# Attention and two MLP layers on one core: q and k loaded two pairs ahead, and the shared tile's scores on the column halves of TensorE

## The chip, the cores and the metric

The kernel runs on one core of one Trainium2 chip. The metric is the device time of one execution in microseconds (us). The engines are TensorE (PE for its matmuls, PEld for its weight loads), VectorE (DVE), ScalarE (ACT), GpSimd (POOL) and SyncE (SP), which here only issues DMAs.

## The reference, cut to what matters

```python
# q, k, v: (2, 12, 448, 64) float32, i.e. 24 heads of 448 positions and 64 dimensions
scores = q @ k^T / 8                         # per head, causal mask
attn = exp(scores - max) / (sum + 1e-9)
x = attn @ v                                 # -> 896 tokens x 768
h = x @ w_in;  g = max(h, 0) + alpha * min(h, 0);  x = g @ w_out     # d_ff = 2048, weights in float64
h = x @ w_in2; g = 0 below -1, h above 1, (h + 1)^2 / 4 between;  out = g @ w_out2
```

## The kernel before, in words

The heads are worked in 12 pairs. Pair `p` has one tile `qk_raw` (128 partitions: 64 dimensions of each of its two heads; q and k side by side). The 448 query rows of a head are three tiles of 128 and a rest of 64. The two rests of a pair share one tile of 128 rows, the "shared tile": its scores come from `qdiag`, a 128x128 block-diagonal of the two heads' last 64 queries, against all of `k` (line 372). `qk_raw` has three buffers that go round, and so has `qdiag`; `v` has five.

The loop of line 489 is a pipeline written out by hand. In its turn `p` it issues, in this order: the scores of pair `p` (query tiles 0 and 1, then the shared tile), their exponentials, attention times v of pair `p-2` (`attnv`, lines 446 and 454, which writes each head to one half of the partitions), its evacuation to `x`, one step of preparing the first MLP weights (from turn 3 on, `prime`), transposes of pair `p-1` (line 430), scores and exponentials of query tile 2, more transposes, and the division by the sums (`norm`: POOL, with one reciprocal on DVE). Every engine executes its instructions in the order in which they were issued. The scores of a turn go into banks `s0` and `s1`, which DVE empties into `pexp` (line 383); the transposes go into banks that ACT and DVE empty together (line 439).

DMAs of q, k, v and of the weights are all issued by SP in the order of the code, apart from half of pair 0. At the end of turn `p` (lines 523 to 529) come q and k of pair `p+1`, with two small DMAs for its `qdiag`, then v of pair `p+1` in seven DMAs, and in turn 1 the first two weight chunks of 768 KB each (line 103). The first step of `prime` is `magnitude` (ACT, line 113), which reads weight chunk 0 in turn 3; chunk 1 is read by the same step in turn 9.

After the loop four MLP layers follow (`run_layer`, line 253 makes all of their products, in three passes of split weights and inputs). Turns 12 and 13, which have no scores, already mix in products of layer 1.

Of the kernel before, what the change touches and what calls it, by code (L numbers as in the profile page):

```python
# [22 lines left out]
def attention_moe_moe_kernel(ctx: ExitStack, tc: tile.TileContext, qk, v, w1, w2, w3, w4, alpha, out):  # L23
# [8 lines left out]
    nc = tc.nc  # L32
    NP, _, _, S = qk.shape
    NB = 2
    CP, D = v.shape[1], v.shape[-1]
# [30 lines left out]
    def warm_up():  # L66

        z = const.tile([128, 512], F32R, tag="zero", name="zero")
        nc.vector.memset(f32(z), 0.0)
        for _ in range(NWARM):  # L70
            ps = ps_o.tile([128, 512], F32, tag="o", name="warm_ps")
            nc.tensor.matmul(ps, lhsT=z[:, :128], rhs=z, start=True, stop=True)

    def constants():
        nc.vector.memset(half, 0.5)
        make_identity(nc, ident)
        for t, p0, n in ((mask, 0, Q), (mask_rest, 0, D), (mask_rest, D, D)):
            if p0 == 0:
                nc.gpsimd.memset(t, 0.0)
            d = t[p0:p0 + n, t.shape[1] - n:]  # L80
            nc.gpsimd.affine_select(
                out=d, in_=d, compare_op=ALU.is_ge, fill=MASK, base=0, pattern=[[-1, n]], channel_multiplier=1
            )


    class Weights:
# [82 lines left out]
        def next(self):  # L169
            self.n_used += 1  # L170
            return self.split.pop(self.n_used - 1)
# [66 lines left out]
    def new_banks():  # L238

        pools = (ps_s, "s0"), (ps_s, "s1"), (ps_s, "s2"), (ps_o, "o"), (ps_t, "t0"), (ps_t, "t1"), (ps_t, "t0"), (ps_t, "t1")  # L240
        while True:
            for pool, tag in pools:
                yield pool.tile([128, 512], F32, tag=tag, name="ps")
# [17 lines left out]
    def early_tiles(batches):  # L261

        for f, bs in enumerate(batches):
            ws = wts.next()
            ps = {b: new_tile() for b in bs}
            early[f] = ws, ps
            for k in range(KD - 1):
                products(ps, ws, x_t, k, k, k == 0, False)
                yield

    def run_layer(layer, late):

        if layer in (1, 3):
            mt, nch, kc, src = NF, 1, KD, x_t
        else:
            mt, nch, kc, src = NM, NC2, KC, g_t
        evac = {1: act_prelu, 2: evac_x, 3: act_quad, 4: evac_out}[layer]
        for m in range(mt):
            ps = {}
            for ch in range(nch):  # L280
                if layer == 1 and m in early:
                    ws, ps = early.pop(m)
                    products(ps, ws, src, kc - 1, kc - 1, False, True)
                else:
                    ws = wts.next()
                rest = {b: new_tile() for b in range(NB) if b not in ps} if ch == 0 else ps

                end = layer == 4 and m == mt - 1 and ch == nch - 1
                for group in [{b: p} for b, p in rest.items()] if end else [rest] if rest else []:
                    for k in range(kc):  # L290
                        kk = ch * kc + k
                        products(group, ws, src, k, kk, kk == 0, kk == nch * kc - 1)
                    if end:
                        interleave(*(evac(p, m, b) for b, p in group.items()), [])
                ps = {**ps, **rest}
                if wts.n_used > 1 and not early:
                    interleave(wts.split_ops(), late)
                    late = []
                    wts.load()
                    wts.magnitude()  # L300
            late = [] if end else [op for pair in zip(*(evac(ps[b], m, b) for b in range(NB))) for op in pair]
        return late


    class Attention:
# [51 lines left out]
        def scores(self, p, tiles):  # L357
            if 0 in tiles:
                self.pexp[p] = self.ap.tile([Q, 2, TRI], F32, tag="pexp", name="pexp", bufs=3)
                self.st[p] = self.ap.tile([Q, 2, 2 * NQ + 1], F32, tag="stat", name="stat", bufs=4)  # L360
            t = self.raw[p]
            if NQ in tiles:
                banks = [self.ps_s.tile([128, 512], F32, tag="s2", name="rest_ps")]
            else:
                banks = [self.ps_s.tile([128, 512], F32, tag=f"s{j}", name=f"s{j}_ps") for j in range(2)]
            off, todo = 0, []
            for i in tiles:
                for n, (e, col) in enumerate(self.rows(p, i)):
                    w = e.shape[1]
                    ps = banks[n][:, off:off + w]  # L370
                    if i == NQ:
                        nc.tensor.matmul(ps, lhsT=self.qdiag[p % 3], rhs=t[:, 1, :], start=True, stop=True)
                        todo.append((e, ps, mask_rest, col))
                    else:
                        h = slice(n * D, (n + 1) * D)
                        nc.tensor.matmul(  # L376
                            ps, lhsT=t[h, 0, i * Q:(i + 1) * Q], rhs=t[h, 1, :w], start=True, stop=True
                        )
                        todo.append((e, ps, mask[:, REST - w:], col))
                off += w  # L380

            for e, ps, m, col in todo:
                nc.vector.tensor_tensor_reduce(  # L383
                    out=e, in0=ps, in1=m, scale=-SCALE, scalar=3.0e38, op0=ALU.add, op1=ALU.min,
                    accum_out=self.st[p][:, 0, col:col + 1],
                )
# [76 lines left out]
    with tc.manual_schedule():  # L463
        wts = Weights()
        ps_s, ps_t, ps_o = (
            ctx.enter_context(tc.tile_pool(name=f"ps_{n}", bufs=b, space=PSUM))
            for n, b in (("s", 1), ("t", 2), ("o", 1))
        )
        banks = new_banks()
        with ExitStack() as pa:  # L470
            ap = pa.enter_context(tc.tile_pool(name="attn", bufs=2))
            at = Attention(ap, ps_s, ps_t, ps_o)
            at.zeros()
            at.load(0)
            warm_up()
            at.load(1)
            at.load_v(0)
            nc.sync.dma_start(out=alpha_sb, in_=alpha)
            constants()
            early = {}  # L480
            fill = early_tiles(((0, 1), (0,)))
            prime = wts.prime()
            PRIME = 3

            for p in range(NP + 2):
                new, mid, old = p < NP, 1 <= p <= NP, p >= 2  # L490

                def spare():
                    if not new:
                        next(prime, None)
                        next(fill, None)

                if new:
                    at.scores(p, (0, 1))
                    at.scores(p, (NQ,))
                    at.expo(p, (0, 1, NQ))  # L500
                spare()
                if old:
                    at.attnv(p - 2)
                    high, low = at.evac(p - 2)
                    high()
                if p >= PRIME:
                    next(prime, None)
                if mid:
                    at.transp(p - 1, (0, 1))
                if new:  # L510
                    at.scores(p, (2,))
                if old:
                    low()
                if new:
                    at.expo(p, (2,))
                spare()
                if mid:
                    at.transp(p - 1, (NQ,))
                    at.transp(p - 1, (2,))
                if new:  # L520
                    at.norm(p)
                spare()
                if 0 < p < NP - 1:
                    at.load(p + 1)
                if p + 1 < NP:
                    at.load_v(p + 1)
                if p == PRIME - 2:
                    wts.load()
                    wts.load()
            for _ in fill:  # L530
                pass
            for _ in prime:
                pass
        gpool = ctx.enter_context(tc.tile_pool(name="g", bufs=1))
        ep = ctx.enter_context(tc.tile_pool(name="ep", bufs=2))
        late = []
        for layer in (1, 2, 3, 4):
            late = run_layer(layer, late)
            if layer % 2 == 0:
                interleave(late, [])  # L540
                late = []
# [44 lines left out]
```

## Time and profile before

| | |
|---|---|
| median of 3 runs | 563.89 us (562.46 to 571.53) |
| the profiled execution's own time | 563.78 us |
| its span, first to last instruction | 561.9 us |
| PE / DVE / ACT / POOL busy | 97% / 74% / 43% / 24% of the span |
| mean granted TensorE clock | 0.993 of full speed |

A row of the trace below gives start and duration in us, the engine, the line and operation, what it writes and reads, how many instructions were merged into it, and in brackets how long the engine had been idle before and what ended that. "SPq" rows are DMA issues: their duration is the time to issue, not to transfer. One float32 matmul of the code appears as two records (two passes).

### The profile page before, as it was taken

The page shows a single profiled execution, that of the slowest core. Times are in us where ns is not written, and L with a number is a line of the kernel's source. Part 1 is how long each engine was busy: PE and PEld are TensorE (multiplying, and loading weights), DVE is VectorE, ACT ScalarE, POOL GpSimd, SP SyncE. Part 2 cuts the span into 40 slices and gives each one's busy share as a digit, 9 for nine tenths or more (in the row PEclk, how much of TensorE's full clock was granted, in tenths as well). Part 3 has the DMA queues.
Part 4 walks back from the last instruction along what each step waited for, and adds up shares of the span by engine and source line. Part 5 has one row for each costly group of instructions (what it writes and reads, how often), then busy time and mean ns, then how long its engine had stood idle before and what let it go on. Part 6 is the DMA issues. An engine that isn't in the chain of part 4 may idle for free.

```text
span 561.9 us, 8739 instructions
## 1 busy us (share of the span) xinstructions
PE 547.4 (97%) x3195; PEld 482.2 (86%) x3195; DVE 418.4 (74%) x797; ACT 240.6 (43%) x509; POOL 136.6 (24%) x179
## 2 busy tenths in 40 slices
PE   7699999999999999999999999999999999999997
PEld 3456667999999999999999999999999999999996
DVE  4569886888888998765765779888888867555740
ACT  5578984333333333322233345555555433222220
POOL 4526753133333331000000003333333300000000
PEclk9889999999999999999999999999999999999999
DMA  4544511333333223433333523333322244343421
GB/s 122 199 136 117 167 55 58 112 113 113 113 113 113 75 76 113 127 98 113 114 112 88 177 97 108 113 113 113 113 95 75 76 129 143 132 130 128 145 71 33
DMA packets 25674, 62.31 MB, mean 111 GB/s; under 512 B 5280, under 2 KB 13984, under 8 KB 25632
## 3 DMA queue, kind: packets, MB, share of 16 engines
q1 hardware_dynamic: 23760, 60.15, 34.5%
q10 hardware_dynamic: 1872, 1.61, 0.8%
q8 instruction: 25, 0.41, 0.3%
q14 instruction: 17, 0.14, 0.1%
HBM read 58.99 MB, written 2.75 MB: 110 GB/s over the span
## 4 chain that ended last, share of the span: by engine, by line
PE 84%; POOL 0%; DVE 0%; ACT 0%; issue 0%; ACTq 0%
PE ps L253 83%; PE o_ps L446 0%; PE t_ps L430 0%; POOL pexp L403 0%; PE o_ps L454 0%; DVE o_sb L226 0%; ACT o_sb L226 0%; ACTq L226 0%
## 5 line engine op out<-in xcount | busy, mean ns | idle before, releaser
L253 PE MATMUL ps<-x,w_split 128*128 128x448 f32 x1152 | 234.7, 366 | 0.0
L253 PE MATMUL ps<-g,w_split 128*128 128x448 f32 x1152 | 233.8, 365 | 0.0
L253 PEld LDWEIGHTS ps<-g,w_split 128*128 128x128 f32 x1152 | 216.3, 188 | 17.1
L253 PEld LDWEIGHTS ps<-x,w_split 128*128 128x128 f32 x1152 | 216.0, 188 | 17.4
L177 POOL TENSOR_TENSOR g<-act_g,g 128x448 fp32r<-128x448 f32 x64 | 85.5, 1336 | 271.3 <-ACT g L176 271.2
L150 ACT CAST w_split<-w_f 128x512 fp32r<-128x512 f32 (+1 forms) x80 | 56.6, 707 | 125.8 <-DVE w_f L147 86.7
L153 DVE TENSOR_TENSOR w_split<-w_f,w_split 128x512 fp32r<-128x512 f32 (+1 forms) x80 | 66.1, 827 | 52.6 <-ACT w_split L150 52.5
L176 ACT CAST g<-act_g 128x448 fp32r<-128x448 f32 x64 | 36.2, 565 | 76.8 <-DVE act_g L189 62.8
L129 DVE TENSOR_SCALAR w_f<-w_f 128x512 f32<-128x512 f32 (+1 forms) x80 | 58.5, 731 | 9.0 <-ACT w_f L113 8.9
L147 DVE SCALAR_TENSOR_TENSOR w_f<-w_raw,w_f 128x512 uint32<-128x512 uint32 (+1 forms) x80 | 63.6, 795 | 1.4
L141 DVE SCALAR_TENSOR_TENSOR w_f<-w_raw,w_f 128x512 uint32<-128x512 uint32 (+1 forms) x80 | 63.5, 794 | 1.4
L113 ACT ACTIVATE w_f<-w_raw 128x512 f32<-128x512 f32 (+1 forms) x80 | 61.2, 764 | 0.4 <-DMA w_raw<-w 0.4
L392 ACT ACTIVATE pexp<-pexp,stat 128x128 f32<-128x128 f32 (+2 forms) x72 | 35.8, 499 | 16.8 <-DVE stat L383 16.5
L135 DVE TENSOR_SCALAR w_f<-w_f 128x512 uint32<-128x512 uint32 (+1 forms) x80 | 38.2, 478 | 1.4
L201 ACT ACTIVATE act_t<-act_t,half 128x448 f32<-128x448 f32 x32 | 21.5, 672 | 37.7 <-DVE act_t L200 37.7
L403 POOL TENSOR_SCALAR pexp<-pexp,stat 128x128 f32<-128x128 f32 (+2 forms) x72 | 34.5, 494 | 4.7 <-DVE stat L383 3.3
L383 DVE CUSTOM_DVE_ANT_0 pexp<-s_ps,mask 128x128 f32<-128x128 f32 (+2 forms) x72 | 26.2, 413 | 9.6 <-PE s_ps L376 9.2
L376 PE MATMUL s_ps<-qk_raw 64*128 64x128 f32 (+2 forms) x144 | 25.4, 431 | 5.6 <-DMA qk_raw<-qk 4.8
L226 DVE COPY o_sb<-ps 128x224 f32<-128x224 f32 x12 | 4.7, 391 | 29.8 <-ACT o_sb L226 29.8
L439 DVE COPY pt<-t_ps 128x128 f32<-128x128 f32 (+2 forms) x36 | 14.0, 418 | 13.1 <-PE t_ps L430 13.1
L446 PEld LDWEIGHTS o_ps<-pt,v 128*64 128x64 f32 x144 | 9.7, 143 | 14.9 <-ACT pt L439 6.0
L200 DVE TENSOR_SCALAR act_t<-ps 128x448 f32<-128x448 f32 x32 | 19.9, 622 | 3.0 <-PE ps L253 2.4
(47 smaller groups left out, 280.4 us busy)
## 6 DMA issues: line engine op xcount, KB each, us to landing
w_raw<-w SPq DMA_DIRECT2D x32, 768.0 KB, 4.3
w_raw<-w SPq DMA_DIRECT2D x48, 512.0 KB, 3.7
qk_raw<-qk SPq DMA_DIRECT2D x11, 448.0 KB, 3.9
out<-o_sb SPq DMA_DIRECT2D x12, 112.0 KB, 1.7
out<-o_sb ACTq DMA_DIRECT2D x12, 112.0 KB, 1.7
v<-v SPq DMA_DIRECT2D x12, 56.0 KB, 2.7
v<-v SPq DMA_DIRECT2D x12, 48.0 KB, 2.1
v<-v SPq DMA_DIRECT2D x12, 40.0 KB, 2.0
```

The lines of the kernel that those rows point to most:

```text
L113: nc.scalar.activation(out=f32(w), in_=f32(hi), func=AF.Abs)
L129: nc.vector.tensor_scalar(out=f32(w), in0=f32(w), scalar1=HI_MIN, scalar2=HI_MAX, op0=ALU.max, op1=ALU.min)
L135: nc.vector.tensor_scalar(out=w, in0=w, scalar1=5, scalar2=2, op0=ALU.logical_shift_left, op1=ALU.logical_shift_right)
L141: nc.vector.scalar_tensor_tensor(out=w, in0=hi, scalar=0xC0000000, in1=w, op0=ALU.bitwise_and, op1=ALU.bitwise_or)
L147: nc.vector.scalar_tensor_tensor(out=w, in0=lo, scalar=29, in1=w, op0=ALU.logical_shift_right, op1=ALU.bitwise_or)
L150: nc.scalar.copy(s[:, 0, :n], f32(w))
L153: nc.vector.tensor_sub(s[:, 1, :n], f32(w), f32(s[:, 0, :n]))
L176: nc.scalar.copy(t[:, 0, :], g)
L177: nc.gpsimd.tensor_sub(t[:, 1, :], g, f32(t[:, 0, :]))
L253: nc.tensor.matmul(ps[b][:, :S], lhsT=ws[:, part, k * 128:(k + 1) * 128], rhs=src[b, kk][:, xp, :], start=first and part == 0 and xp == 0, ...
L392: nc.scalar.activation(out=e, in_=e, func=AF.Exp, bias=st[:, 0, col:col + 1], scale=-1.0, accum_out=st[:, 1, col:col + 1],)
L403: nc.gpsimd.tensor_scalar(out=e, in0=e, scalar1=sums[:, col:col + 1], scalar2=1.0, op0=ALU.mult, op1=ALU.mult)
```

## The change

At the end of turn `p` the kernel now issues q and k of pair `p+2` instead of `p+1`, from turn 0 on; v stays one pair ahead. The first two weight chunks are issued one each in turns 1 and 2, behind q, k and v of that turn, where both were issued in turn 1. Second, the one matmul of the shared tile's scores is made as two, each with one half of the columns of `qdiag` (one head), each writing one half of the partitions.

```diff
@@ scores
                     if i == NQ:
-                        nc.tensor.matmul(ps, lhsT=self.qdiag[p % 3], rhs=t[:, 1, :], start=True, stop=True)
+                        for j in range(2):
+                            h = slice(j * D, (j + 1) * D)
+                            nc.tensor.matmul(
+                                ps[h], lhsT=self.qdiag[p % 3][:, h], rhs=t[:, 1, :], start=True, stop=True
+                            )
                         todo.append((e, ps, mask_rest, col))
@@ the loop over pairs
                 spare()
-                if 0 < p < NP - 1:
-                    at.load(p + 1)
+                if p + 2 < NP:
+                    at.load(p + 2)
                 if p + 1 < NP:
                     at.load_v(p + 1)
-                if p == PRIME - 2:
-                    wts.load()
+                if p in (PRIME - 2, PRIME - 1):
                     wts.load()
```

SP's instructions before, from q and k of pair 2 on (`qk_raw_275` is pair 2, `qk_raw_393` pair 3; `v2_88` is v of pair 2; `w_raw` are weight chunks):

```order
L336 DMA qk_raw_275<-qk 128x896
L340 DMA qdiag2_85<-qk 64x64 x2
L348 DMA v2_88<-v 112x128
L348 DMA v2_88<-v 16x128
L348 DMA v2_88<-v 96x128
L348 DMA v2_88<-v 32x128
L348 DMA v2_88<-v 80x128
L348 DMA v2_88<-v 48x128
L348 DMA v2_88<-v 64x128
L103 DMA w_raw_286<-w1 128x1536
L103 DMA w_raw_288<-w1 128x1536
L336 DMA qk_raw_393<-qk 128x896
```

Pair 3 is issued behind v of pair 2 and two weight chunks. The same place of SP's order now (`qk_raw_281` is pair 3, `qk_raw_398` pair 4):

```order
L336 DMA qk_raw_281<-qk 128x896
L340 DMA qdiag0_83<-qk 64x64 x2
L348 DMA v2_88<-v 112x128
L348 DMA v2_88<-v 16x128
L348 DMA v2_88<-v 96x128
L348 DMA v2_88<-v 32x128
L348 DMA v2_88<-v 80x128
L348 DMA v2_88<-v 48x128
L348 DMA v2_88<-v 64x128
L103 DMA w_raw_292<-w1 128x1536
L336 DMA qk_raw_398<-qk 128x896
```

Pair 3 now stands ahead of v of pair 2 and of every weight chunk, and it is pair 4 that follows one chunk.

PE's instructions at the head of turn 3, before (`s_ps` are scores, `rest_ps` the shared tile, `o_ps` attention times v of pair 1):

```order
L376 MATMUL s_ps<-qk_raw 128x128 x2
L376 MATMUL s_ps<-qk_raw 128x256 x2
L372 MATMUL rest_ps<-qk_raw,qdiag_83 128x448
L446 MATMUL o_ps<-pt,v_87 64x2x3x64 x2
L446 MATMUL o_ps<-pt,v_87 64x2x2x64 x2
```

and now, five lines further down in the code:

```order
L381 MATMUL s_ps<-qk_raw 128x128 x2
L381 MATMUL s_ps<-qk_raw 128x256 x2
L375 MATMUL rest_ps<-qk_raw,qdiag_83 64x448 x2
L451 MATMUL o_ps<-pt,v_87 64x2x3x64 x2
L451 MATMUL o_ps<-pt,v_87 64x2x2x64 x2
```

One matmul of 128 rows of output became two of 64, in the same place, and nothing else moved on PE.

## Rows read from the trace of the kernel before

**Rows 1.** The chain that ended last: start, us, what.

```profile
96.13 462.29 PE ps L253 x2280
```

**Rows 2.** Stretches: busy us of each engine, then granted clock, DMA share, GB/s.

```profile
20.00:25.00 5.00, 1.36 (x24) 0.90 (x22) 3.10 (x10) 2.48 (x9) 2.18 (x7) 1.00 0.88 340
25.00:30.00 5.00, 3.89 (x12) 1.75 (x14) 1.61 (x9) 1.84 (x8) 1.64 (x3) 0.52 0.42 117
```

**Rows 3.** PE in order of time: turns 2 to 5, then 9 to 11.

```profile
16.51 1.02 PE L372 MATMUL rest_ps<-qk_raw,qdiag 128*128 128x448 f32 x2
...
20.75 0.61 PE L430 MATMUL t_ps<-ident,pexp 64*128 64x64 f32 x12
26.11 1.65 PE L376 MATMUL s_ps<-qk_raw 64*128 64x128 f32 x8 [4.75 <-DMA qk_raw<-qk]
27.69 1.86 PE L372 MATMUL rest_ps<-qk_raw,qdiag 128*128 128x448 f32 x2
...
35.92 1.02 PE L372 MATMUL rest_ps<-qk_raw,qdiag 128*128 128x448 f32 x2
...
42.05 1.02 PE L372 MATMUL rest_ps<-qk_raw,qdiag 128*128 128x448 f32 x2
...
66.75 1.02 PE L372 MATMUL rest_ps<-qk_raw,qdiag 128*128 128x448 f32 x2
...
73.14 1.02 PE L372 MATMUL rest_ps<-qk_raw,qdiag 128*128 128x448 f32 x2
...
79.27 1.02 PE L372 MATMUL rest_ps<-qk_raw,qdiag 128*128 128x448 f32 x2
```

**Rows 4.** SP in order of time: issues of v, q and k, and weights.

```profile
8.27 3.27 SPq L348 DMA_DIRECT2D v<-v  x7
11.59 0.58 SPq L336 DMA_DIRECT2D qk_raw<-qk  x1
...
13.45 3.43 SPq L348 DMA_DIRECT2D v<-v  x7
16.92 1.07 SPq L103 DMA_DIRECT2D w_raw<-w  x2
18.09 0.45 SPq L336 DMA_DIRECT2D qk_raw<-qk  x1
...
20.79 6.03 SPq L348 DMA_DIRECT2D v<-v  x7
```

**Rows 5.** Last line of the view of line 336: its DMAs, issue to landing.

```profile
DMA to landing us min/median/max: 3.5/3.9/7.9
```

**Rows 6.** Last line of the view of tile `w_raw`, first 100 us.

```profile
DMA to landing us min/median/max: 4.2/4.6/7.1
```

**Rows 7.** Turn 5, in order of time: PEld waiting for DVE, DVE waiting for PE.

```profile
41.20 0.52 PEld L376 LDWEIGHTS s_ps<-qk_raw 64*128 64x128 f32 x6 [0.18 <-DVE stat L383]
...
45.57 0.62 DVE L439 COPY pt<-t_ps 128x128 f32<-128x128 f32 x2 [0.78 <-PE t_ps L430]
```

**Rows 8.** PE in very short stretches of turn 5: single records, and what follows.

```profile
42.53 0.54 PE L372 MATMUL rest_ps<-qk_raw,qdiag 128*128 128x448 f32 x1
43.00 0.54 PE L446 MATMUL o_ps<-pt,v 128*64 128x384 f32 x2
...
43.00 0.87 PE L446 MATMUL o_ps<-pt,v 128*64 128x384 f32 x4
```

**Rows 9.** PEld there in order of time.

```profile
43.37 0.14 PEld L446 LDWEIGHTS o_ps<-pt,v 128*64 128x64 f32 x2 [0.18 <-issue]
```

**Rows 10.** Turns 6, 7 and 9 in order of time: waiting transposes, and ACT's weight step.

```profile
53.00 0.52 PE L430 MATMUL t_ps<-ident,pexp 64*128 64x64 f32 x10 [0.19 <-POOL pexp L403]
...
59.30 0.68 PE L430 MATMUL t_ps<-ident,pexp 64*128 64x64 f32 x12 [0.60 <-POOL pexp L403]
...
70.38 0.92 ACT L113 ACTIVATE w_f<-w_raw 128x768 f32<-128x768 f32 x1
...
71.82 0.68 PE L430 MATMUL t_ps<-ident,pexp 64*128 64x64 f32 x12 [0.67 <-issue]
```

## The prediction

> **What bounds the kernel now.** First the chain that ended last: from 96.13 us on it is one piece, 2280 matmuls of the MLP layers with no gap, to the end of the work [rows 1]. So nothing after 96 us can be gained or lost by this change, unless it makes the weights late, and each microsecond that the attention part ends sooner or later moves the end by one microsecond.
>
> Next the busy time by stretches of 5 us over the attention part. One stretch stands out: from 20 to 25 us PE is busy for 1.36 us, while the DMA engines are 88% busy; in the next the granted clock has fallen to a mean of 0.52, that is, to the lower of its two levels, 1.2 GHz [rows 2]. PE in order of time shows what happened. It finished turn 2's transposes at 21.36 (20.75 + 0.61) and next ran the scores of pair 3 at 26.11, 4.75 us later, released by the DMA of q and k; the shared tile's scores, which follow, took 1.86 us instead of 1.02 [rows 3]. The step from one turn's shared tile to the next's is a clean yardstick: 42.05 - 35.92 = 6.13 us undisturbed, but 27.69 - 16.51 = 11.18 from turn 2 to 3 and 35.92 - 27.69 = 8.23 from turn 3 to 4 [rows 3].
>
> SP's order says why the DMA was late. Pair 3 was issued at 18.09, right behind two weight chunks at 16.92 [rows 4], and took 7.9 us to land, the longest of all q and k loads against a median of 3.9 [rows 5]: 18.09 + 7.9 = 26.0, which is where PE starts.
>
> Then what sets the 6.13 us. In turn 5 DVE stands idle for 0.78 us until PE's transposes are done, then copies them and empties the banks of query tile 2's scores; PE's next scores wait for that [rows 7]. After them PE runs the shared tile, attention times v and the transposes, on which DVE waits again. The shared tile lies on this loop, though not in every turn: in turns 6 and 7 the last transposes wait for POOL (0.19 and 0.60 us), in turn 9 they wait (0.67 us) behind ACT, whose order now holds the 0.92 us weight step of line 113 [rows 10].
>
> **The loads, step by step.** SP reaches pair 3 sooner: v of pair 1 began at 8.27, and pair 2, which took its place behind that at 11.59, now stands ahead of it. q, k and `qdiag` cost SP 13.45 - 11.59 = 1.86 us, v of a pair some 3.3 [rows 4]. So pair 2 is issued at 8.3, v of pair 1 at 10.1, pair 3 at about 13.4. Its buffer is that of pair 0, whose last scores PE makes before turn 1's shared tile, which stood a step ahead of 16.51, near 10.4; so SP does not wait for it. Even the longest landing gives 13.4 + 7.9 = 21.3 [rows 5], just when PE comes free at 21.36; a median one gives 17.3. Step 2 to 3 then is a normal 6.13: 11.18 - 6.13 = 5.05 us gained. In step 3 to 4 the clock stays at its upper level, but ACT has line 113 in turn 3, as in turn 9, and step 9 to 10 took 73.14 - 66.75 = 6.39 [rows 3, 10]: 8.23 - 6.39 = 1.84. Together **6.9 us**. Bounds: if both steps are 6.13, 7.2; if both are 6.39, 6.6.
>
> What is moved past what: v of pair 1 comes 1.9 us later, is all issued by 13.4 and is first read in turn 3, beyond 22 us, so hidden. v of pairs 2 and on stands where it stood. Weight chunk 0 comes at about 13.4 + 1.9 + 3.4 = 18.7 instead of 16.9. Its first reader is ACT in turn 3; in turn 9 this step began 70.38 - 66.75 = 3.63 after the shared tile [rows 3, 10], so it is wanted at 16.51 + 6.13 + 3.63 = 26.3. The longest landing of a weight chunk, 7.1 us [rows 6], gives 25.8: hidden, by 0.5 in the worst case. If that cover goes, ACT waits ahead of the copies that PE's transposes need, one for one. Chunk 1 comes some 6 us after chunk 0, at about 24.5, and is wanted in turn 9. Pair 4, issued right behind chunk 0 at 19.2, lands at 27.1 at the worst; turn 4 wants it at 21.4 + 6.4 = 27.8. Later SP runs a pair ahead and waits for PE to free the buffer of pair `p-1`; behind that wait stand v and the later chunks, each with turns to spare. What is late next in turn 3 is thus nothing on DMA, but DVE's emptying of the banks, as in every turn.
>
> **The halves, step by step.** Today the shared tile's two passes begin at 42.05 and 42.53, and attention times v at 43.00: 0.95 us of path [rows 3, 8]. Attention times v is already made on column halves. Its records of 384 columns come two side by side, and the second two end 0.87 - 0.54 = 0.33 us after the first two [rows 8]. By columns, 0.33 x 448 / 384 = 0.385 for each pass of the shared tile on both halves, 0.77 for both passes, with nothing paid between it and the attention matmuls, which stand in the same arrangement. That is **0.18 us less** on the loop of a turn. The weight loads double in number (four for two); their cover is the matmuls themselves, as with the two loads of 0.14 us that run at 43.37 under the matmuls of 43.00 to 43.87 [rows 8, 9].
>
> The step is followed by attention times v in ten turns, 2 to 11. In turns 3 and 9 ACT, in 6 and 7 POOL ends the wait last, and I count nothing there: 6 x 0.18 = **1.1 us**. Bounds: 0, if POOL, ACT and DVE take it up everywhere, and 10 x 0.18 = 1.8. I take 1.1, since DVE's 0.78 us of idle time in turn 5 says that it does have room.
>
> **The sum.** 6.9 + 1.1 = 8.0. The profiled execution took 563.78 us (span 561.9 and 1.9 around it), within 0.1 of the median of the three runs: 563.8 - 8.0 = **555.8 us**, 1.4% less.
>
> **Rivals.** *The halves give nothing.* POOL's division and ACT's copies stand 0.2 to 0.7 us behind PE in three turns of [rows 10]; a faster PE may only wait longer for them. For it: these waits. Against: the six turns without one. 563.8 - 6.9 = 556.9.
>
> *The weight loads of the halves are bare.* If none could run beside a matmul, each of the four pieces would have a load of 0.14 ahead of it: 0.77 + 0.56 = 1.33 for 0.95, or 10 x 0.38 = 3.8 lost: 563.8 - 6.9 + 3.8 = 560.7. Against: the loads at 43.37. The Trainium skill ("TensorE: Matmul & The Clock Gate", Part 3, The mechanism) states such a rule: a weight load overlaps a running matmul only where the two use different row groups, and the two halves here use the same rows. By that rule it would come out so; the trace differs, with loads under running matmuls of just this shape.
>
> *The halves run one after the other,* each as long as the shared tile today: 1.90 for 0.95, in ten turns 9.5 us, and the kernel is slower than before: 563.8 - 6.9 + 9.5 = 566.4. It decides from 6.9 / 10 = 0.69 us more per turn on. For it: both halves stream the same `k`, which no matmul pair here does. Against: the side-by-side records of [rows 8].
>
> *Pair 3 is late still,* since more small DMAs of v stand just ahead of it, or SP is held up: at half the loss (3.4 us) 560.3. Against: it needs a landing beyond 7.9 us with no weight chunk in the way.
>
> **Chances.** Forecast 0.60; halves give nothing 0.17; loads bare 0.05; one after the other 0.04; pair 3 late 0.04; both terms at their upper bounds, 563.8 - 9.0 = 554.8, or a little under, 0.10. The range takes in the forecast, the first and the last case. Its ends are the bounds of both terms, 554.8 and 563.8 - 6.6 = 557.2, each widened by 1.4 us, the distance of the fastest run from the median of those shown, to 553.4 and 558.6; I take 553.2 to 559.0. About 2% (11.3 us, below 552.6) is what a measurement of this kernel can tell from no change, and no case above goes that far either way: faster 0.05, the same 0.92, slower 0.03, where the tails stand for mechanisms that I have not seen.
>
> **What would show it.** Right: no idle PE between 21 and 26 us, granted clock 1.00 from 20 us on, q and k landing within some 5 us, turn 3's shared tile near 22.6 and turn 4's near 29; the last piece of the chain beginning near 88; the shared tile 0.77 us ahead of attention times v, with four records in two side-by-side pairs. Wrong: ACT waiting for `w_raw` in turn 3, transposes waiting longer for POOL, or a step between shared tiles of 6.13 still, which would make the halves worth nothing.

## The result, and the profile after

The changed kernel took 0.9869 of the time of the kernel before (95% interval 0.9846 to 0.9891). Its profiled execution took 555.52 us, span 553.7, where the one before took 563.78: 8.3 us less, against 8.0 forecast (555.8); by the ratio, over more executions, it is 1.3% less, against 1.4% forecast. Some executions of the kernel before, of the changed one and of others here are some 9 us longer or more, in the profiled ones because the 2280 matmuls of the MLP layers take 471.40 us instead of 462.29 at the same granted clock, and no run here tells why: ratios and ranges leave them out, and four profiles of this kind (the halves alone, v in two DMAs on the changed kernel, and both of the last version) are read for their attention part only.

The chain of waits of the changed kernel, its last long piece:

```profile
87.89 462.29 PE ps L253 x2280
```

It is as long as before and begins 96.13 - 87.89 = 8.24 us sooner [rows 1]: the whole gain lies ahead of it. The two stretches by 5 us that stood out before [rows 2], now:

```profile
20.00:25.00 5.00, 5.00 (x62) 3.22 (x60) 4.60 (x20) 4.29 (x17) 2.68 (x7) 1.00 0.78 272
25.00:30.00 5.00, 4.13 (x58) 2.67 (x56) 3.97 (x17) 4.81 (x17) 2.35 (x6) 1.00 0.50 150
```

PE is busy throughout the first, and the clock never leaves its upper level. PE in order of time, the rows that answer to [rows 3] and [rows 8]:

```profile
16.57 0.97 PE L375 MATMUL rest_ps<-qk_raw,qdiag 128*64 128x448 f32 x4
...
22.50 0.97 PE L375 MATMUL rest_ps<-qk_raw,qdiag 128*64 128x448 f32 x4
...
27.56 0.68 PE L435 MATMUL t_ps<-ident,pexp 64*128 64x64 f32 x12 [0.87 <-issue]
...
28.88 0.97 PE L375 MATMUL rest_ps<-qk_raw,qdiag 128*64 128x448 f32 x4
...
34.82 0.97 PE L375 MATMUL rest_ps<-qk_raw,qdiag 128*64 128x448 f32 x4
35.62 1.46 PE L451 MATMUL o_ps<-pt,v 128*64 128x384 f32 x12
...
71.23 0.97 PE L375 MATMUL rest_ps<-qk_raw,qdiag 128*64 128x448 f32 x4
```

Steps between shared tiles: turn 2 to 3 5.93 us (11.18 in [rows 3]), 3 to 4 6.38 (8.23), 4 to 5 5.94 (6.13). The shared tile now has four records, two side by side, and attention times v follows 0.80 us after its start, not 0.95. Turn 5 in very short stretches, first two of the records and then the four weight loads, done at 35.02 while those run:

```profile
34.82 0.60 PE L375 MATMUL rest_ps<-qk_raw,qdiag 128*64 128x448 f32 x2
...
34.82 0.20 PEld L375 LDWEIGHTS rest_ps<-qk_raw,qdiag 128*64 128x64 f32 x4 [0.33 <-DMA v<-v]
```

SP in order of time, for [rows 4], and the landing of q and k from the view of line 336, for [rows 5]:

```profile
8.29 0.43 SPq L336 DMA_DIRECT2D qk_raw<-qk  x1
...
13.52 0.53 SPq L336 DMA_DIRECT2D qk_raw<-qk  x1
...
19.05 1.38 SPq L103 DMA_DIRECT2D w_raw<-w  x1
20.52 0.38 SPq L336 DMA_DIRECT2D qk_raw<-qk  x1
...
27.32 0.39 SPq L336 DMA_DIRECT2D qk_raw<-qk  x1
...
34.05 0.35 SPq L336 DMA_DIRECT2D qk_raw<-qk  x1
...
40.54 0.53 SPq L336 DMA_DIRECT2D qk_raw<-qk  x1
...
46.12 0.53 SPq L336 DMA_DIRECT2D qk_raw<-qk  x1
```

```profile
DMA to landing us min/median/max: 3.0/4.0/5.4
```

Pair 3 was issued at 13.52, 7.7 us before its scores. But the later pairs are not a turn ahead: pair 7 was issued at 40.54 and its scores began at 45.94, 5.4 us later, which is just the longest landing; pair 8 came 5.58 us after it.

### The profile page after: what moved, and what is told of

Its sections match the earlier page's. It is cut to its first block, busy times and chain, and to the rows that moved or that the text cites. A ratio compares the mean times of both kernels' runs of the same rounds, so it can differ in the third digit from the quotient of the medians.

```text
span 553.7 us, 8785 instructions
## 1 busy us (share of the span) xinstructions
PE 543.2 (98%) x3219; PEld 480.8 (87%) x3219; DVE 418.2 (76%) x797; ACT 239.8 (43%) x509; POOL 136.8 (25%) x179
## 4 chain that ended last, share of the span: by engine, by line
PE 85%; POOL 0%; DVE 0%; ACT 0%; issue 0%; ACTq 0%
PE ps L253 84%; PE o_ps L451 0%; PE t_ps L435 0%; POOL pexp L408 0%; PE o_ps L459 0%; DVE o_sb L226 0%; ACT o_sb L226 0%; ACTq L226 0%
## 5 line engine op out<-in xcount | busy, mean ns | idle before, releaser
L381 PE MATMUL s_ps<-qk_raw 64*128 64x256 f32 (+2 forms) x144 | 25.1, 425 | 0.7 <-DVE stat L388 0.7
L184 DVE TENSOR_SCALAR act_t<-ps,alpha_sb 128x448 f32<-128x448 f32 x32 | 21.5, 672 | 0.1
```

## The experiments

**Each part alone.** The loads only (the shared tile undone):

```diff
-                        for j in range(2):
-                            h = slice(j * D, (j + 1) * D)
-                            nc.tensor.matmul(
-                                ps[h], lhsT=self.qdiag[p % 3][:, h], rhs=t[:, 1, :], start=True, stop=True
-                            )
+                        nc.tensor.matmul(ps, lhsT=self.qdiag[p % 3], rhs=t[:, 1, :], start=True, stop=True)
```

> Only the loads are changed; the shared tile is one matmul of 128 columns, as before. If the two parts simply add, as the prediction has it: 6.9 us less than the kernel before, 556.9 us by the profile (span about 555.0), shared-tile steps of 6.13 us from turn 2 to 3 and about 6.39 from 3 to 4, undisturbed steps still 6.13. If the loads are worth something only together with the halves: above 558.5 us.

Measured: 0.989 of the time before (0.9874 to 0.9907), 556.66 us profiled. PE in order of time:

```profile
16.29 1.02 PE L372 MATMUL rest_ps<-qk_raw,qdiag 128*128 128x448 f32 x2
...
22.42 1.02 PE L372 MATMUL rest_ps<-qk_raw,qdiag 128*128 128x448 f32 x2
...
28.82 1.02 PE L372 MATMUL rest_ps<-qk_raw,qdiag 128*128 128x448 f32 x2
34.95 1.02 PE L372 MATMUL rest_ps<-qk_raw,qdiag 128*128 128x448 f32 x2
```

Steps of 6.13, 6.40 and 6.13: the term of the loads as it was worked out.

The halves only (the kernel before with the new lines 372 to 376):

> Only the halves are changed; q and k one pair ahead and both weight chunks in turn 1, as before. If the halves pay by themselves: undisturbed steps of 5.94 us instead of 6.13, the steps 2 to 3 and 3 to 4 still around 11 and 8, in all about 1 to 1.3 us less than before, 562.5 to 562.8 us. If they pay only where the loads are early: 563.8 us.

Measured: 0.9976 (0.9966 to 0.9985), 562.19 us median. Compared at like granted clock, with the runs of the kernel before on that chip, the means differ by 1.1 us (0.991 to 0.994) and 1.6 us (0.996 and 0.997). The attention part of the profile has undisturbed steps of 5.94 us, and turn 3 still waits.

```profile
26.40 1.65 PE L380 MATMUL s_ps<-qk_raw 64*128 64x128 f32 x8 [4.86 <-DMA qk_raw<-qk]
...
34.91 0.97 PE L374 MATMUL rest_ps<-qk_raw,qdiag 128*64 128x448 f32 x4
40.85 0.97 PE L374 MATMUL rest_ps<-qk_raw,qdiag 128*64 128x448 f32 x4
46.79 0.97 PE L374 MATMUL rest_ps<-qk_raw,qdiag 128*64 128x448 f32 x4
```

So each part pays by itself and they add: 0.989 x 0.9976 = 0.9866.

**Which part of the new load order counts.** Both chunks in turn 1 again, the rest as changed:

```diff
-                if p in (PRIME - 2, PRIME - 1):
+                if p == PRIME - 2:
+                    wts.load()
                     wts.load()
```

> The changed kernel, but with both weight chunks issued in turn 1 again, behind v of pair 2; pair 4 then stands behind two chunks, where pair 3 stood before. If only the place of pair 3 matters: pair 4 is issued near 21 us and lands by 28 to 29, turn 4 wants it at 28.05, so 0 to 1 us more than the changed kernel, 555.5 to 556.5 us. If spreading the chunks over two turns is what pays: turn 4 waits for pair 4 as turn 3 did for pair 3, 3 us or more, 558.5 us or more.

Measured: 557.65 us, between the two. Step 3 to 4 took 7.67 us (6.38 as changed): pair 4, issued at 20.85, reaches 28.45 with this run's longest landing, 7.6 us, and its scores began at 28.63, though the view puts that wait down to DVE. And PE waited 1.58 us in a turn that nobody had named:

```profile
72.49 0.93 PE L381 MATMUL s_ps<-qk_raw 64*128 64x128 f32 x8 [1.58 <-DMA qk_raw<-qk]
```

This is pair 11, over 45 us after the chunks. One pair ahead, with the chunks moved behind pairs 3 and 4:

```diff
-                if p == PRIME - 2:
-                    wts.load()
+                if p in (PRIME - 1, PRIME):
                     wts.load()
```

> The kernel before (one pair ahead, one matmul for the shared tile), but with the two weight chunks issued in turns 2 and 3, one each, behind q, k and v of that turn. If what counts is that pair 3 stands ahead of the chunks: pair 3 is issued at 16.9 us and lands near 21, turn 3 starts on time or under 0.6 us late, and ACT waits at most 1 us for chunk 0: 556.9 to 558.5 us. If a lead of two pairs is needed: turn 3 still waits 2 us or more for pair 3, above 559.5 us.

Measured: 561.2 us, the second alternative by its total, though turn 3 itself was only 0.59 us late. PE and ACT in order of time:

```profile
21.77 0.93 PE L376 MATMUL s_ps<-qk_raw 64*128 64x128 f32 x8 [0.59 <-DMA qk_raw<-qk]
...
28.07 0.89 ACT L113 ACTIVATE w_f<-w_raw 128x768 f32<-128x768 f32 x1 [1.86 <-DMA w_raw<-w]
...
37.04 0.93 PE L376 MATMUL s_ps<-qk_raw 64*128 64x128 f32 x8 [1.39 <-DMA qk_raw<-qk]
...
69.74 0.93 PE L376 MATMUL s_ps<-qk_raw 64*128 64x128 f32 x8 [1.18 <-DMA qk_raw<-qk]
```

The waits are spread over the whole attention part. That pointed away from the two chunks alone and to SP, which in both kernels issues ten DMAs a pair. So the same kernel again, with v of a pair laid out in memory so that two DMAs bring it (in `load_v`):

```diff
-            k = 0
-            while k < S:
-                (c, r), (d, u) = divmod(k, Q), divmod(k, CP)
-                n = min(Q - r, CP - u)
-                nc.sync.dma_start(out=t[r:r + n, c], in_=v[p, u:u + n, d])
-                k += n
+            n = Q * NQ * 2 * D
+            nc.sync.dma_start(out=t[:, :NQ], in_=v[p, :n].rearrange("(r c j d) -> r c j d", r=Q, c=NQ, j=2))
+            nc.sync.dma_start(out=t[:D, NQ], in_=v[p, n:].rearrange("(r j d) -> r j d", r=D, j=2))
```

> The run with one pair ahead and the chunks in turns 2 and 3, with v of a pair in two DMAs instead of seven. If its late turns waited for q and k because SP, with ten DMAs a pair, issues them too late: no PE wait for q and k over 0.2 us any more, and ACT's wait for chunk 0 (1.86 us) mostly gone, 556.5 to 557.5 us. If one pair of lead is too little whatever SP does: the waits of turns 5, 7 and 10 stay, above 559 us.

Measured: 556.15 us, no wait of PE for q and k or of ACT for a chunk left, 5.05 us less for five DMAs fewer a pair; these are single executions, but their profiles agree, with the last piece of the chain beginning at 93.59 and at 88.56. That is as fast as the loads-only kernel above, without the second pair of lead in the code. The other layout also means fewer packets (7213 against 11246 in the first 90 us), so this run does not separate fewer issues from fewer packets. What it does show is that q and k landed no sooner after their issue (median 4.4 us against 4.0): they were issued sooner. SP now does run ahead, until a buffer is not free (it waits for PE for 22.7 us in 8 waits): in its order of time the issues are a turn apart, with pair 5 at 19.98 for its shared tile at 34.40, and pairs 6 and 7 behind it:

```profile
19.98 0.33 SPq L336 DMA_DIRECT2D qk_raw<-qk  x1
...
26.11 0.33 SPq L336 DMA_DIRECT2D qk_raw<-qk  x1
...
32.49 0.33 SPq L336 DMA_DIRECT2D qk_raw<-qk  x1
```

The same edit on the changed kernel:

> The changed kernel with v of a pair in two DMAs instead of seven (another layout of v in memory). If SP's issuing of some 6.2 us per turn only just keeps up in the changed kernel but costs it nothing: the time stays at 555.3 to 555.7 us, while q and k of each pair are issued over 8 us before their turn instead of 5.4 to 7.7. If it costs something already: below 555.0 us.

Measured, in the attention part: it ends at 87.51 us, against 87.89, with the same steps (5.94, 6.38, 5.94 ...) and pair 7 issued at 32.51, against 40.54. SP cost the changed kernel nothing in that profiled execution. But in another execution of the very same changed kernel it did:

> The changed kernel itself, on the same chip: 555.5 us, 0.6 to 1.0 us above the one with v in two DMAs and ACT's steps moved; from turn 2's shared tile to the last piece of the chain 71.3 us.

Measured: 0.9891 (0.9871 to 0.9911), 555.22 to 558.58 us; the profiled one took 556.54 and shows two waits and what stands behind the first:

```profile
27.06 0.58 SPq L103 DMA_DIRECT2D w_raw<-w  x1
27.74 0.38 SPq L336 DMA_DIRECT2D qk_raw<-qk  x1
...
34.29 0.93 PE L381 MATMUL s_ps<-qk_raw 64*128 64x128 f32 x8 [1.31 <-DMA qk_raw<-qk]
...
70.92 0.93 PE L381 MATMUL s_ps<-qk_raw 64*128 64x128 f32 x8 [0.51 <-DMA qk_raw<-qk]
```

Pair 5, right behind the second chunk, was issued 0.4 us later than in the first profile and took 6.4 us to land instead of at most 5.4. PE was also early: turn 2's shared tile began at 15.91, 0.66 us sooner than in the first profile, so part of the two waits is that lead given back, and the last piece of the chain began 1.05 us later (88.94). The expectation of a fixed 555.5 us fell: the changed kernel sits at the edge.

**Where the halves save.** The shared tile first in each turn, so that attention times v no longer follows it, once with halves and once with one matmul:

```diff
-                    at.scores(p, (0, 1))
                     at.scores(p, (NQ,))
-                    at.expo(p, (0, 1, NQ))
+                    at.scores(p, (0, 1))
+                    at.expo(p, (NQ, 0, 1))
```

> The changed kernel with the shared tile's scores, their reduction and their exponentials ahead of those of query tiles 0 and 1 in each turn. The shared tile then fills PE's wait for DVE's banks and leaves the loop of PE and DVE. If that loop is the only limit of a turn: undisturbed steps of 5.6 to 5.7 us instead of 5.94, about 552.5 us. If SP, which issues a pair's DMAs in about 6.2 us, is the next limit: PE waits for q and k again in late turns, the turns stay near 5.9 to 6.2, 554 to 556 us.

> The same order with the shared tile as one matmul on all 128 columns, so that it differs from the run before it only in the halves, and in neither does attention times v follow the shared tile. If the halves save because nothing is paid between the shared tile and attention times v: no difference here, the shared tile to the next scores within 0.05 us of the halves. If they save in the tile itself, by shorter weight loads: 0.1 to 0.2 us longer from the shared tile's start to the next scores' start than with halves.

Measured: 559.57 us with halves, 559.11 with one matmul. With halves it is the longer by what happened up to turn 3's shared tile (at 23.63 us against 22.95), where its granted clock averaged 0.66 from 15 to 20 us; from there to the last piece of the chain it is 0.22 us shorter (68.31 against 68.53). From shared tile to the next scores, PE in order of time, first with halves, then without:

```profile
36.49 0.97 PE L375 MATMUL rest_ps<-qk_raw,qdiag 128*64 128x448 f32 x4
37.40 0.93 PE L381 MATMUL s_ps<-qk_raw 64*128 64x128 f32 x8
```

```profile
35.85 1.02 PE L372 MATMUL rest_ps<-qk_raw,qdiag 128*128 128x448 f32 x2
36.80 0.93 PE L376 MATMUL s_ps<-qk_raw 64*128 64x128 f32 x8
```

0.91 against 0.95: away from attention times v the halves are worth 0.04 us, next to it 0.95 - 0.80 = 0.15. So, by the difference, most of the saving is what was not paid between the two, not the tile itself. As a faster kernel the order failed, and not in the way that either expectation had it: the undisturbed step did fall, to 5.78 us, without any wait for q and k, but the seven steps from turn 4 to 11 took 43.51 us against 42.35 in the changed kernel. In turn 7, for one, the transposes waited 0.93 us and began at 54.98, when ACT, held up by the cast of line 150, had made its copy (to 54.88). Why these waits grow is read from the trace, not tested.

**What the long turns wait for.** ACT's step of line 113 moved behind its first copy of transposes, turns 3 and 9:

```diff
-                if p >= PRIME:
+                if p >= PRIME and p not in (3, 9):
                     next(prime, None)
                 if mid:
                     at.transp(p - 1, (0, 1))
+                if p in (3, 9):
+                    next(prime, None)
```

> The changed kernel with ACT's weight step of line 113 issued behind ACT's first copy of transposes in turns 3 and 9, instead of ahead of it. If this step is what makes the steps 3 to 4 and 9 to 10 long (6.38 and 6.37 us): both fall to 5.94 to 6.1, 0.6 to 0.9 us less in all, 554.6 to 554.9 us. If it is the DMAs of these turns: both stay at 6.4, 555.5 us.

Measured: 555.37 us. Steps 3 to 4 and 9 to 10 fell to 5.93, but the steps after them rose from 5.94 to 6.11, so the two places gained 0.28 and 0.27 us, 0.55 in all, just short of the expectation; that ACT's 0.9 us still does not fit into its idle time would explain it, and was not tested. From turn 2's shared tile to the last piece of the chain 70.80 us, against 71.32.

Then both that and v in two DMAs, and in turn 7 ACT's cast of line 150 moved in the same way:

```diff
-                nc.scalar.copy(s[:, 0, :n], f32(w))
+                high = lambda: nc.scalar.copy(s[:, 0, :n], f32(w))
+                high() if self.defer is None else self.defer.append(high)
```

> The changed kernel with v in two DMAs, ACT's step of line 113 behind the first copy of transposes in turns 3 and 9, and its cast of line 150 likewise in turn 7. If ACT's order is what lengthens these three turns: steps 3 to 4 and 9 to 10 near 6.1, 7 to 8 down from 6.25 to between 5.95 and 6.15, from turn 2's shared tile to the last piece of the chain 0.6 to 0.9 us less than in the changed kernel, 554.6 to 554.9 us. If POOL is what turn 7 waits for, as the prediction had it: step 7 to 8 stays at 6.25, 555.0 us.

> The kernel with v in two DMAs and ACT's three weight steps behind the first copy, again, for a profile and a ratio beside the changed kernel on one chip: 553.9 to 554.8 us, span about 552.5, from turn 2's shared tile to the last piece of the chain 70.5 us.

Measured: 0.9812 (0.971 to 0.9914) in the first set of runs; in the second, on the chip of the last run of the changed kernel, 0.9855 (0.984 to 0.987), 553.81 to 554.77 us, where the changed kernel had 555.22 to 558.58. The attention part, from turn 2's shared tile to the last piece of the chain, took 70.51 us in either profile, against 71.32 and, with the two waits, 73.03 in the changed kernel. PE in order of time in the second:

```profile
46.51 0.97 PE L374 MATMUL rest_ps<-qk_raw,qdiag 128*64 128x448 f32 x4
...
52.44 0.97 PE L374 MATMUL rest_ps<-qk_raw,qdiag 128*64 128x448 f32 x4
58.57 0.97 PE L374 MATMUL rest_ps<-qk_raw,qdiag 128*64 128x448 f32 x4
```

Step 7 to 8 is 5.93 instead of 6.25, with POOL's work untouched: it was ACT that turn 7 waited for (and again part of it, 6.13 for 5.94, is given back one step later). This is the fastest version here.

## Why the prediction was right, point by point

- **What bounds the kernel** held: nothing after 96 us moved but its start.
- **The loads, 6.9 us.** The first profile gives 11.18 + 8.23 before and, without the halves, 6.13 + 6.40: 6.9. Against the runs it is a little less, 563.11 to 556.88, or 6.2: among the 13 runs of the kernel before on that chip, times go from 562.53 at a mean granted clock of 0.997 to 563.92 at 0.993, and the prediction read its loss from an execution at 0.993. So there is some luck in how near 555.8 the first profile came: another execution of the same changed kernel took 558.58.
- **The halves, 1.1 us.** Measured 1.4, a small miss of size: seven steps from turn 4 to 11 gained 43.35 - 42.35 = 1.0, step 2 to 3 0.20 more than the loads alone, and the way from turn 11's shared tile to the MLP layers 0.20 (16.66 against 16.86). A full step gained 0.19 to 0.20, not 0.18: the tile takes 0.80 and not 0.77 us to attention times v, but attention itself (1.46 for 1.52) starts without a pause. Turns 6 and 7, counted at nothing, gave 0.14 and 0.06; turns 3 and 9 gave at most 0.02, as counted. The loads of the weight halves did run beside matmuls: the rival of bare loads would have given 1.33 us where 0.80 was measured. The Trainium skill ("TensorE: Matmul & The Clock Gate", Part 3, The mechanism) states that a weight load overlaps a running matmul only where the two use different row groups. This trace differs: the four loads of turn 5 are done at 35.02, under matmuls that began at 34.82.
- **Turn 7 waits for POOL** was wrong, and a sign of being wrong that the prediction had named did show: these transposes wait 0.74 us now, 0.60 before. The view named POOL, which ended at about the same time; ACT's cast of line 150 had pushed the copy that frees the banks:

```profile
50.30 1.14 POOL L408 TENSOR_SCALAR pexp<-pexp,stat 128x384 f32<-128x384 f32 x2
50.31 0.83 ACT L150 CAST w_split<-w_f 128x768 fp32r<-128x768 f32 x1
...
51.05 0.53 ACT L444 COPY pt<-t_ps 128x128 f32<-128x128 f32 x2
...
51.67 0.68 PE L435 MATMUL t_ps<-ident,pexp 64*128 64x64 f32 x12 [0.74 <-POOL pexp L408]
```

  (the changed kernel, turn 7, in order of time: POOL ended at 51.44, ACT's copy at 51.58, and PE began at 51.67.) The rival that the halves give nothing leaned on this reading.
- **"Later SP runs a pair ahead and waits for PE"** was the step that failed, without a cost in the first profile. SP hardly gets ahead: from one pair's issue to the next's it takes 5.2 to 6.7 us for ten DMAs, 6.4 to 7.0 with a chunk, and a turn is now 5.94. The shortest step, 13.52 - 8.29 = 5.23, is one in which SP waits for nothing; over the attention part it waits three times for DMAs of q and k while it issues v, and little for PE (SP's waits to 80 us in the changed kernel: us in all, times, longest):

```profile
SPq L348 <- DMA qk_raw<-qk: 3.3, 3, 1.1
SPq L336 <- PE t_ps L435: 1.1, 3, 0.4
```

  Why an issue of v waits there is open. The two chunks made pair 3 late, as forecast, but the 4.75 us stall also gave SP the lead from which all later turns of the kernel before were fed: pair 4 was issued at 26.91 there, 8.2 us before its scores at 35.09. Take the stall away at one pair of lead, and the waits come back all over (561.2 us); take five issues a pair away from SP, and one pair is enough (556.15). The second pair of lead in the change is thus not needed against the chunks, once these come a turn later and one at a time; it pays for SP's slowness, and barely.

## What to carry to other kernels

A stall hides whatever was about to become late. Before removing one, work out for every queue that it feeds what a turn costs there, issue time included, and compare it with the new, shorter turn; here SP with ten issues a pair was the next limit, and v in two larger DMAs was worth as much as a second pair of lead (556.15 us against 556.66). Where a small matmul stands next to others made on halves of the array, making it on halves too saved 0.2 us each time; away from them it saved 0.04.

## What the runs showed that was not expected

- The kernel before has two close groups of times, 562.3 to 563.1 us at a mean clock of 0.996 or 0.997 and 563.1 to 564.3 at 0.992 or 0.993: how much time the clock spends at its lower level differs between executions. When it falls differs too. In the profile before, the lower level lasts from about 25 to 32 us; with only the halves it lasts from about 23 to 30, so that more of it falls into the stall, and step 3 to 4 took 6.93 us there instead of 8.23. The stretches of the run with only the halves (1.00 and 0.80 before):

```profile
20.00:25.00 5.00, 1.54 (x24) 0.98 (x22) 3.10 (x10) 2.70 (x9) 2.67 (x8) 0.81 0.89 333
...
30.00:35.00 5.00, 4.54 (x74) 3.33 (x72) 3.14 (x11) 4.33 (x14) 0.08 (x1) 1.00 0.55 141
```
